# Forty-eight of the 128 half rows of the last up-projection slice, loaded as nine short transfers

## The chip, the cores and the metric

The kernel runs on one core of one Trainium2 chip. The metric is the device time of one execution in microseconds, lower is better. The core has a matrix engine (PE, with weight loads shown as PEld), a vector engine (DVE), a scalar engine (ACT), a general engine (POOL), and a sequencer (SP) that issues nearly all transfers of this kernel. Transfers from HBM to the on-chip memory are carried out by 16 DMA engines. The on-chip memory has 128 partitions; the kernel holds one array, `space`, of 50,176 32-bit columns on every partition, and manages it by itself.

## The reference

Two attention blocks and two gated MLP blocks alternate, with the same weights both times, for a batch of two and one new token:

```
x = x + attention(layernorm(x))      # 32 heads of 128, 8192 cached keys and values per head, width 576
x = x + mlp(layernorm(x))            # h = gelu(x @ w_gate) * (x @ w_up);  h @ w_down;  inner width 4608
x = x + attention(layernorm(x))
x = x + mlp(layernorm(x))
```

All of it is float32. Keys and values are 537 MB together and are read in both attention blocks, except what is held on chip from one to the next. The second MLP, where the change lies, needs the 576 x 4608 matrices `w_gate` and `w_up` and the 4608 x 576 matrix `w_down`, 10.6 MB each.

## The kernel before, in words

**One queue of loads.** The function `plan_first`, `plan_mlp(0)`, `plan_second` and `plan_mlp(1)` write the list of all loads in the order in which they are to be issued. Each entry of the list, `queue`, is a function that looks for a place in `space` (class `Arena`) and, if there is one, issues the transfer on SP's queue; if not, it returns False and the list stops there. `done(key)` frees a place and calls `pump`, which goes on with the list. All this happens while the program is written, so that the order of the issues is fixed; on the chip SP waits, before each issue, until the last readers of the place are done. The method `Arena.fit` tries the end of the last place it gave, then a lower bound, then the ends of all places in use.

**Completion semaphores.** The transfers on SP's queue take eight completion semaphores in turn. Before a transfer is issued on a semaphore, SP waits until the transfer that had it before, eight issues earlier, has landed.

**The second MLP.** `plan_mlp(1)` puts these loads on the list behind the eight 128-row blocks of the second output projection (`wo`): `w_gate` in two transfers, `w_up` in four, `w_down` in seven. A weight matrix of 576 rows of 4608 is seen as 1152 half rows of 2304 values (9216 bytes). Partition `p` holds half rows `9p` to `9p + 8`; `half_rows` loads for all 128 partitions the slices `us` of these nine. `GU` says which: `w_gate` slices 0 to 4 and 5 to 8, `w_up` slices 0 to 2, 3 to 5, 6 and 7, and, alone, slice 8. That last one, the ninth half rows of the up projection, is one transfer of 128 rows of 9216 bytes.

**The products.** `norm` writes the normalised input to the tile `xt`, with 32 columns for each of the nine slices: a half row belongs to the first or the second half of the weight's columns, by whether partition and slice are even or odd, and the input stands once for each half (columns multiplied by `side`). `all_products` then goes through the slices in the order of the loads; for each slice it makes eight products, of eight columns of `xt` with 288 columns of the weight, which add up in the two banks of the accumulator `acc`. PE has to wait for each transfer as it comes to it. Then `activate` (scaling by `rstd`, a transpose, the gelu) is run for each of the two banks, and the products with `w_down` follow in the order of its seven transfers. Ahead of the first four of these, `idle_products` makes a few products whose results are not used. `add_to_x` and two small stores end the program.

```
GU = [[range(0, 5), range(5, NU)], [range(0, 3), range(3, 6), range(6, 8), single[-1]]]
...
nc.sync.dma_start(t.rearrange("p (u w) -> p u w", w=width), rows[:, us[0]:us[-1] + 1, :])
```

Of the kernel before, what the change touches and what calls it, by code (L numbers as in the profile page):

```python
# [11 lines left out]
ALU = mybir.AluOpType  # L12
AX = mybir.AxisListType
PSUM = bass.MemoryType.PSUM

P = 128
B = 2
# [4 lines left out]
DF = 4608  # L22
# [3 lines left out]
HALF = P // 2  # L26

GH = 4
NU = 9
EQ = 512  # L30
HG = DF // 16
PAD = 6
# [10 lines left out]
END = RING + NPLACE * PLACE  # L43
HELD = 5
SPLIT = (18, 18, 12, 16)
FOLD = 2


# [76 lines left out]
def decode_layers(ctx, tc, x_in, kc, vc, wq, wo, wg, wu, wd, out):  # L125
    nc = tc.nc
# [12 lines left out]
    for c in range(4):  # L139
        for s in range(2):  # L140
            lo = 32 * c + s * B
# [5 lines left out]
    arena = Arena()  # L147
    queue, ready, places = [], {}, {}

    def pump():  # L150
        while queue and queue[0]():
            queue.pop(0)

    def done(key):
        arena.free(key)
        pump()

    def part_at(at, n):
        return space[:, at:at + n]
# [62 lines left out]
    def by_rows(key, src, n, k, loaded):  # L222

        first, rows = sum(SPLIT[:k]), SPLIT[k]

# [24 lines left out]
    def half_rows(key, w, us, first):  # L250

        width = w.shape[1] // 2
        rows = w.rearrange("r (s w) -> (r s) w", w=width).rearrange("(p u) w -> p u w", p=P)

        def transfers(t):
            nc.sync.dma_start(t.rearrange("p (u w) -> p u w", w=width), rows[:, us[0]:us[-1] + 1, :])

        weights(key, len(us) * width, first, transfers)

    def of_half(h, k):  # L260

        width = wq.shape[1] // 2
        rows = wq.rearrange("r (s w) -> (r s) w", w=width).rearrange("(p u) w -> p u w", p=P)

        def transfers(t):
            for e in range(2):
                nc.sync.dma_start(t[e::2, :], rows[e::2, 2 * k + (h + e) % 2, :])

        weights(("wq", 1, h, k), width, None, transfers)
# [63 lines left out]
    GU = [[range(0, 5), range(5, NU)], [range(0, 3), range(3, 6), range(6, 8), single[-1]]]  # L333
# [87 lines left out]
    def plan_mlp(layer):  # L421
        if layer == 0:
            for h in range(2):
                for u in range(4):
                    split_rows("g", wg, h, u)
                split_middle(h)
                for u in range(4):
                    split_rows("u", wu, h, u)
        else:
            for g, (name, w) in enumerate((("g", wg), ("u", wu))):  # L430
                for us in GU[g]:
                    half_rows((name, layer, us[0]), w, us, 0)
        for rows in DOWN[layer]:
            down(layer, rows)

# [7 lines left out]
    ident = consts.tile([P, P], F32, name="ident")  # L443
# [48 lines left out]
    home = consts.tile([P, 3 * DH + 16], F32, name="home")  # L492
# [3 lines left out]
    xt = consts.tile([P, PAD + NU * 32], F32, name="xt")  # L496
# [3 lines left out]
    acc = psum1.tile([P, 2, 512], F32, name="acc")  # L500
# [12 lines left out]
    low = bank2[:, 2 * GH + P + 8:]  # L513
    share = low[:, :FOLD * JC]
    kept = psum1.tile([P, JC, DH], F32, name="kept")
# [15 lines left out]
    def small(p, n):  # L531

        if n > 2:
            return turned[0:p, 0:n]
        smalls.append(smalls.pop(0))
        return smalls[0][0:p, 0:n]
# [65 lines left out]
    def attention(layer):  # L602
# [75 lines left out]
        def split(n):  # L678

            return layer == 1 and n == SINGLE[1]  # L680

        def count(n, k, m):

            return SPLIT[k] if split(n) else m * JC

        def base(n, k):

            return sum(SPLIT[:k]) if split(n) else k * JC

# [17 lines left out]
        def multiply(n, k, m):  # L707
# [7 lines left out]
            if n == SINGLE[1] and k == 0 and layer == 0:  # L715
                rest = ready[key_of(n)][2].rearrange("p j d -> p (j d)")[:, (JC - SPLIT[2]) * DH:]
                for to, lo in (
# [143 lines left out]
        def weigh(n):  # L861

            lo = ITEMS[n].parts - FOLD
            pr = weights_of(n)[:, 2 * JC * lo:2 * JC * (lo + FOLD)].rearrange("p (g a e) -> p a g e", a=2, e=4)
            nc.vector.tensor_tensor(
                out=share.rearrange("p (g e) -> p g e", e=4), in0=pr[:, 0], in1=pr[:, 1], op=ALU.add
            )
            rows = FOLD * JC
            t = part_at(arena.live[name("v", layer, n), lo][0], FOLD * PART).rearrange("p (j d) -> p j d", d=DH)
            nc.vector.tensor_tensor(out=t, in0=t, in1=share.unsqueeze(2).to_broadcast([P, rows, DH]), op=ALU.mult)  # L870
# [4 lines left out]
        def folded(n):  # L875

            key, lo = name("v", layer, n), ITEMS[n].parts - FOLD
            nc.tensor.matmul(  # L878
# [198 lines left out]
    def mlp(layer):  # L1077
        split = layer == 0
        rstd = norm(split)
        if split:  # L1080
            idle_products(2, 1)
        hT = once.tile([P, 2, NI, 2, 2, B], F32, name="hT", tag="xc")

        def window(u, at):

            return xt[:, PAD + 32 * u - at:PAD + 32 * u - at + 4 * B]

        def split_products(h):

            steps = [(("g", layer, h, u), u, 2, (0,)) for u in range(4)] + [(("gu", layer, h), 4, 1, (0, 1))]  # L1090
            steps += [(("u", layer, h, u), u, 2, (1,)) for u in range(4)]
            for key, u, sides, gs in steps:
                w = ready.pop(key).rearrange("p (k c w) -> p k c w", c=4, w=HG)
                for k in range(2):
                    g, e = (k, 0) if u == 4 else (gs[0], k)
                    for c in range(4):
                        nc.tensor.matmul(
                            acc[32 * c:32 * c + 4 * B, h, :HG], window(u, 4 * g + 2 * e), w[:, k, c, :],
                            start=(key == steps[0][0] and k == 0), stop=(key == steps[-1][0] and k == 1),
                        )  # L1100
                done(key)
                if key != steps[-1][0]:
                    idle_products(1, None if h else 1)

        def all_products():

            for g, name in enumerate("gu"):
                for us in GU[g]:
                    w = ready.pop((name, layer, us[0])).rearrange("p (u v c w) -> p u v c w", v=2, c=4, w=HG)
                    for u in us:  # L1110
                        for v in range(2):
                            for c in range(4):
                                nc.tensor.matmul(
                                    acc[32 * c:32 * c + 4 * B, v, :HG], window(u, 4 * g), w[:, u - us[0], v, c, :],
                                    start=(g == 0 and u == 0), stop=(g == 1 and u == NU - 1),
                                )
                    done((name, layer, us[0]))

        def activate(v):

            o = acc[:, v, :HG]
            nc.scalar.activation(o, o, AF.Copy, scale=rstd)  # L1122
            gu = once.tile([P, NI, 32], F32, name="gu", tag="row")
            nc.vector.transpose(gu, o.rearrange("p (m i) -> p i m", i=NI))  # L1124
            g = gu[:, :, 0:4]
            a = once.tile([P, NI, 4], F32, name="ga", tag="part")
            nc.vector.tensor_mul(a, g, g)
            nc.vector.tensor_scalar(a, a, 0.044715, 1.0, op0=ALU.mult, op1=ALU.add)
            nc.vector.tensor_mul(a, a, g)
            nc.scalar.activation(a, a, AF.Tanh, scale=math.sqrt(2.0 / math.pi))  # L1130
            nc.vector.scalar_tensor_tensor(a, a, 1.0, g, op0=ALU.add, op1=ALU.mult)
            nc.vector.tensor_mul(a, a, gu[:, :, 4:8])
            a, to = a.rearrange("p i (e b) -> p (i e) b", b=B), hT[:, v].rearrange("p i e s b -> p (i e) s b")
            nc.vector.tensor_scalar_mul(to[:, :, 0, :], a, 0.5)
            nc.scalar.mul(to[:, :, 1, :], a, 0.5)

        if not split:
            all_products()
        for v in range(2):
            if split:  # L1140
                split_products(v)
            activate(v)
        for n, rows in enumerate(DOWN[layer]):
            if n < len(IDLE[layer]):
                idle_products(IDLE[layer][n], 0)
            w = ready.pop(("d", layer, rows[0])).rearrange("p (i c) -> p i c", c=D)
            for k, (t, i) in enumerate(rows):
                v, e = divmod(t, 2) if split else (t % 2, t // 2)
                for c in range(4):
                    nc.tensor.matmul(  # L1150
                        xps[32 * c:32 * c + 2 * B, :], hT[:, v, i, e, :, :].rearrange("p s b -> p (s b)"),
                        w[:, k, c * CW:(c + 1) * CW],
                        start=(rows is DOWN[layer][0] and k == 0), stop=(t, i) == (NT - 1, NI - 1),
                    )
            done(("d", layer, rows[0]))
        add_to_x()
        if layer == 0:
            idle_products(1)
# [34 lines left out]
```

## Time and profile before

| | |
|---|---|
| median of three runs | 2683.82 us (2683.8 to 2685.11) |
| the profiled execution's own time | 2683.47 us |
| its span, from the first to the last instruction | 2681.7 us |
| bytes read | 1152.39 MB, 430 GB/s over the span |
| DVE, POOL, PE, ACT busy | 76%, 58%, 34%, 6% of the span |
| last load landed | about 2677.9 us after the start of the span |

The profile consists of a page (busy time of the engines, the span in 40 slices, DMA queues, the chain of work that ended last, groups of instructions, transfers) and of views that answer for any window of time: a timeline of instructions with the idle time before each and what ended it, the waits of an engine or of SP's queue, and tables by window. In the tables by window the column "DMA share" is the busy share of the 16 DMA engines, so that 1/16 or 0.06 is one engine. A row of the timeline gives the start, the duration, the engine, the line, what is written and read, the shape and the count, and in brackets the idle time before it. A wait is inferred from semaphores. The time of a run and the span differ by some 1.8 us that lie around the span.

### The profile page before, as it was taken

Reading aid. Unit: us, or ns where it says so; the run is one execution under the profiler, and the core shown is the slowest. Engines: PE = TensorE matmul, PEld = TensorE weight load, DVE = VectorE, ACT = ScalarE, POOL = GpSimd, SP = SyncE. Lnnn points to the kernel's source line nnn. Section 1 sums busy time; section 2 is a strip of 40 time slices with the busy share of each in tenths; the row PEclk is TensorE's granted clock in tenths of the full one; section 3 lists DMA queues with packets and bytes.
Section 4 is the critical chain, followed back from the end, with each engine's and each line's share of the span. In section 5 each row is a group of like instructions: output and inputs, shape, how many; then the busy total and the mean of one; then the engine's idle time right before and its main releaser. Section 6 shows DMA issues by size and latency. Waiting matters only on the chain. (4 is left out here: it accounts for less than half of the span.)

```text
span 2681.7 us, 16126 instructions
## 1 busy us (share of the span) xinstructions
PE 912.3 (34%) x6484; PEld 288.9 (11%) x6484; DVE 2027.3 (76%) x979; ACT 166.9 (6%) x797; POOL 1551.8 (58%) x408
## 2 busy tenths in 40 slices
PE   1323332233233233334663333223323323332346
PEld 0100010010001000111221101001000100010012
DVE  4878888888888888867037878888888888888740
ACT  0000000000000000000026000000000000000000
POOL 2546676667666766744028457666766666676520
PEclk8656655665566566566986665566566556655678
DMA  9999999999999999999999999999999999999998
GB/s 422 437 434 428 435 434 433 431 433 433 434 432 434 430 436 434 428 431 427 417 414 426 436 434 429 434 435 434 431 431 435 432 433 434 433 430 436 430 426 382
DMA packets 31498, 1153.44 MB, mean 430 GB/s; under 512 B 3880, under 2 KB 3904, under 8 KB 5696
## 3 DMA queue, kind: packets, MB, share of 16 engines
q1 hardware_dynamic: 31384, 1152.40, 99.8%
q8 instruction: 51, 0.84, 0.1%
q14 instruction: 23, 0.19, 0.0%
q10 hardware_dynamic: 40, 0.01, 0.0%
HBM read 1152.39 MB, written 0.00 MB: 430 GB/s over the span
## 5 line engine op out<-in xcount | busy, mean ns | idle before, releaser
L767 POOL TENSOR_TENSOR space<-space 128x3072 f32<-128x3072 f32 (+4 forms) x221 | 1127.8, 5103 | 474.8 <-DVE space L738 335.1
L738 DVE TENSOR_TENSOR space<-space,bank 128x6144 f32<-128x6144 f32 (+4 forms) x223 | 1111.8, 4987 | 300.4 <-DMA space<-in_A_k_cache_dram 230.6
L770 DVE TENSOR_REDUCE scores<-space 128x48 f32<-128x3072 f32 (+4 forms) x223 | 569.3, 2553 | 91.9 <-POOL space L767 91.7
L873 POOL TENSOR_TENSOR space<-space 128x2048 f32<-128x2048 f32 x144 | 390.0, 2708 | 385.7 <-DVE space L870 362.3
L899 PE MATMUL acc<-space,prz 128*8 128x512 f32 x3328 | 509.6, 776 | 206.6 <-DMA space<-in_A_v_cache_dram 202.5
L653 PE MATMUL bank<-qsb,pick 4*64 4x128 f32 (+1 forms) x256 | 45.4, 432 | 850.9 <-DVE space L738 843.3
L870 DVE TENSOR_TENSOR space<-space,bank 128x4096 f32<-128x4096 f32 x48 | 212.2, 4420 | 1.6
L899 PEld LDWEIGHTS acc<-space,prz 128*8 128x8 f32 x3328 | 98.7, 107 | 559.4 <-issue 356.8
L819 ACT ACTIVATE nbs<-bank 128x2 f32<-128x2 f32 (+1 forms) x68 | 11.6, 171 | 1812.4 <-PE bank L804 1782.8
L921 PE MATMUL bank<-of,wide 128*32 128x2 f32 x512 | 40.9, 202 | 237.9 <-DVE wide L914 237.9
L653 PEld LDWEIGHTS bank<-qsb,pick 4*64 4x64 f32 (+1 forms) x256 | 20.3, 200 | 872.3 <-DVE space L738 855.5
L796 PE MATMUL bank<-ident,m 128*1 128x128 f32 x68 | 21.7, 319 | 242.5 <-DVE m L794 242.3
L575 POOL TENSOR_TENSOR rstd<-ve,mhalf 128x1 f32<-128x1 f32 x4 | 2.2, 550 | 176.0 <-DVE ve L573 176.0
L878 PE MATMUL acc<-space,owner 128*8 128x512 f32 x96 | 89.9, 1039 | 0.0
L1124 DVE STREAM_TRANSPOSE gu<-acc 128x288 f32<-128x288 f32 x4 | 1.9, 483 | 93.2 <-ACT acc L1122 93.2
L921 PEld LDWEIGHTS bank<-of,wide 128*32 128x32 f32 x512 | 35.7, 154 | 326.1 <-DVE wide L914 324.9
L835 PE MATMUL bank<-sums,unit 128*128 128x2 f32 x120 | 35.2, 363 | 86.9 <-ACT prz L827 86.9
L913 DVE TENSOR_TENSOR acc<-acc,diag 128x512 f32<-128x512 f32 x64 | 43.5, 679 | 27.6 <-PE acc L899 27.6
L940 ACT ACTIVATE oT<-bank,rinv 32x8 f32<-32x8 f32 x110 | 28.5, 259 | 381.5 <-PE bank L921 380.8
L827 ACT ACTIVATE prz<-scores,nbs 64x128 f32<-64x128 f32 (+1 forms) x128 | 50.7, 396 | 17.2 <-POOL prz L817 14.4
L760 ACT ACTIVATE space<-space 128x128 f32<-128x128 f32 x164 | 48.4, 296 | 19.4 <-DVE space L738 16.5
L804 PE MATMUL bank<-m,unit 1*128 1x2 f32 (+1 forms) x136 | 38.5, 350 | 25.6 <-DVE m L802 25.6
(100 smaller groups left out, 519.0 us busy)
## 6 DMA issues: line engine op xcount, KB each, us to landing
space<-in_A_k_cache_dram SPq DMA_DIRECT2D x6, 4096.0 KB
space<-in_A_v_cache_dram SPq DMA_DIRECT2D x5, 4096.0 KB
space<-in_A_wo_dram SPq DMA_DIRECT2D x15, 1152.0 KB
space<-in_B_w_gate_dram SPq DMA_DIRECT2D x16, 576.0 KB
space<-in_B_w_up_dram SPq DMA_DIRECT2D x16, 576.0 KB
space<-in_B_w_down_dram SPq DMA_DIRECT2D x8, 1152.0 KB
space<-in_A_v_cache_dram SPq DMA_DIRECT2D x4, 2048.0 KB
space<-in_A_wq_dram SPq DMA_DIRECT2D x16, 512.0 KB
```

The costliest lines, as they stand in the source:

```text
L653: nc.tensor.matmul(qb[n][to, :], pick[32 * c:32 * c + 4, r:r + 1].to_broadcast([4, P // it.heads]), qsb[32 * c:32 * c + 4, (h % 4) * DH:(h ...
L738: nc.vector.tensor_tensor(out=u[:, :r, :], in0=t[:, :r, :], in1=qb[n].unsqueeze(1).to_broadcast([P, r, DH]), op=ALU.mult)
L760: nc.scalar.activation(u[:, j, :], u[:, j, :], AF.Copy, accum_out=S[n][:, base(n, k) + j:base(n, k) + j + 1])
L767: nc.gpsimd.tensor_tensor(out=half, in0=half, in1=u[:, :r, DH // 2:], op=ALU.add)
L770: nc.vector.tensor_reduce(out=S[n][:, base(n, k):base(n, k) + own_rows(n, k, m)], in_=prod.pop((n, k)), axis=AX.X, op=ALU.add)
L827: nc.scalar.activation(pr[at, lo:].rearrange("p (g e) -> p g e", e=4)[:, 0:it.rows // 2:2, :], s[at, :it.rows].rearrange("p (g r) -> p g r ...
L870: nc.vector.tensor_tensor(out=t, in0=t, in1=share.unsqueeze(2).to_broadcast([P, rows, DH]), op=ALU.mult)
L873: nc.gpsimd.tensor_tensor(out=t[:, :rows], in0=t[:, :rows], in1=t[:, rows:2 * rows], op=ALU.add)
L878: nc.tensor.matmul(accumulator(n)[0:8, :], owner.rearrange("p a e -> p (a e)"), part_at(arena.live[key, lo][0], 4 * DH), start=False, stop ...
L899: nc.tensor.matmul(accumulator(n)[32 * c:32 * c + 8, :], pr[:, at:at + 8], t[g // 4][:, g % 4 * 4:g % 4 * 4 + 4, :].rearrange("p j d -> p ...
L913: nc.vector.tensor_tensor(out=q, in0=q, in1=diag.unsqueeze(2).to_broadcast([P, 4, DH]), op=ALU.mult)
L921: nc.tensor.matmul(po[lo:lo + 32, i, :], t[:, i::GH], of, start=True, stop=True)
```

## The change

The ninth half rows of the second up projection are no longer one transfer of 128 rows. Their place in `space` gets twice the columns and 65 more (4673 instead of 2304), and is asked for earlier, right behind the first `w_gate` transfer.

- **Nine short transfers**, six of six rows and three of four rows, take 48 rows, all of odd partitions: the rows 3, 5 and 7 of each group of eight. 44 of these go to another partition, 0 to 63, into a second block of columns (`low`): row `i` of a transfer goes to partition `to + 4 i`. The other four (103, 111, 119, 127) go where they went before. Three of these transfers are issued ahead of each of three large ones: the second `w_gate` transfer and the first two of `w_up`.
- **Two further transfers**, 64 rows (the even partitions) and 16 rows (partitions 1, 9, ..., 121), take the other 80, ahead of the third `w_up` transfer.
- **The input moves along.** `move_down`, after `norm`, builds from pieces of the identity a 128 x 64 matrix (`perm`, in the last 65 columns of the new place) that moves the input of the 44 rows to their new partitions, multiplies it on PE with the input, and copies the result to spare columns of `xt`; a second spare block gets the input with the moved rows set to zero.
- **The products.** `ninth_products` replaces the eight products of slice 8 by sixteen, eight over 128 partitions and eight over 64. The order of the slices in the products stays.

```
+EARLY = 6
...
+    def ninth_rows(key, w, u):
+
+        width = w.shape[1] // 2
+        rows = w.rearrange("r (s w) -> (r s) w", w=width).rearrange("(q u) w -> u q w", u=NU)[u]
+
+        def make():
+            at = arena.fit(key, 2 * width + HALF + 1, 0)
...
+        def some(lo, step, n, to=None):
+            at = slice(lo, lo + step * (n - 1) + 1, step)
+            if to is None:
+                return piece(lambda home, low: nc.sync.dma_start(home[at, :], rows[at, :]))
+            there = slice(to, to + 4 * n - 3, 4)
+            return piece(lambda home, low: nc.sync.dma_start(low[there, :], rows[at, :]))
+
+        queue.append(make)
+        short = [some(8 * EARLY * a + 3 + 2 * k, 8, EARLY, HALF // 2 * a + k) for a in range(2) for k in range(3)]
+        short += [some(99, 8, 4, 3), some(101, 8, 4, HALF // 2 + 3), some(103, 8, 4)]
+        return short, [some(0, 2, HALF), some(1, 8, 16)]
...
-            for g, (name, w) in enumerate((("g", wg), ("u", wu))):
-                for us in GU[g]:
-                    half_rows((name, layer, us[0]), w, us, 0)
+            half_rows(("g", 1, GU[0][0][0]), wg, GU[0][0], 0)
+            short, rest = ninth_rows(("u", 1, NU - 1), wu, NU - 1)
+            for us, name, w in ((GU[0][1], "g", wg), (GU[1][0], "u", wu), (GU[1][1], "u", wu), (GU[1][2], "u", wu)):
+                for piece in short[:3] or rest:
+                    piece()
+                short = short[3:]
+                half_rows((name, 1, us[0]), w, us, 0)
...
+        def move_down():
+
+            at = PAD + 32 * (NU - 1)
+            perm, here = [ready["u", layer, NU - 1][:, DF + lo:DF + hi] for lo, hi in ((0, HALF), (HALF, HALF + 1))]
+            nc.vector.memset(perm, 0.0)
+            for a in range(2):
+                to = perm[:, HALF // 2 * a:HALF // 2 * a + 4 * EARLY].rearrange("p (c i) -> p c i", i=4)
+                of_ident = ident[:, 8 * EARLY * a:8 * EARLY * (a + 1)].rearrange("p (c e) -> p c e", e=8)
+                nc.scalar.copy(to[:, :, 0:3], of_ident[:, :, 3::2])
+                nc.scalar.copy(to[:, 0:4, 3], ident[:, 96:P].rearrange("p (c e) -> p c e", e=8)[:, :, 3 + 2 * a])
+            moved = small(HALF, 2 * B)
+            nc.tensor.matmul(moved, perm, xt[:, at:at + 2 * B], start=True, stop=True)
+            nc.scalar.copy(xt[:HALF, at + 12:at + 16], moved)
+            nc.vector.reduce_sum(here, perm, axis=AX.X)
+            nc.vector.tensor_scalar(here, here, -1.0, 1.0, op0=ALU.mult, op1=ALU.add)
+            nc.vector.tensor_scalar_mul(xt[:, at + 20:at + 24], xt[:, at:at + 2 * B], here)
+
+        def ninth_products():
...
+            for v in range(2):
+                for c in range(4):
+                    to = acc[32 * c:32 * c + 4 * B, v, :HG]
+                    nc.tensor.matmul(to, xt[:, at + 16:at + 24], w[:, 0, v, c, :], start=False, stop=False)
+                    nc.tensor.matmul(to, xt[:HALF, at + 8:at + 16], w[:HALF, 1, v, c, :], start=False, stop=True)
...
         if not split:
+            move_down()
             all_products()
```

More of the change, by code (lines that the diff above doesn't have):

```diff
@@ L258, in half_rows, with piece, run @@
         weights(key, len(us) * width, first, transfers)
+    def ninth_rows(key, w, u):
[3 more added lines that the diff above has]
+            at = arena.fit(key, 2 * width + HALF + 1, 0)
+            if at is None:
+                return False
+            ready[key] = part_at(at, 2 * width + HALF + 1)
+            return True
+        def piece(issue):
+            def run():
+                t = ready[key]
+                issue(t[:, :width], t[:, width:2 * width])
+                return True
+            return lambda: queue.append(run)
+        def some(lo, step, n, to=None):
[8 more added lines that the diff above has]
+        return short, [some(0, 2, HALF), some(1, 8, 16)]
     def of_half(h, k):
@@ L1103, in split_products @@
                     idle_products(1, None if h else 1)
+        def move_down():
[14 more added lines that the diff above has]
+        def ninth_products():
+            key, at = ("u", layer, NU - 1), PAD + 32 * (NU - 1)
+            w = ready.pop(key)[:, :DF].rearrange("p (s v c w) -> p s v c w", s=2, v=2, c=4)
+            for v in range(2):
[3 more added lines that the diff above has]
+                    nc.tensor.matmul(to, xt[:HALF, at + 8:at + 16], w[:HALF, 1, v, c, :], start=False, stop=True)
+            done(key)
         def all_products():
@@ L1108, in all_products @@
                 for us in GU[g]:
+                    if (g, us[0]) == (1, NU - 1):
+                        ninth_products()
+                        continue
                     w = ready.pop((name, layer, us[0])).rearrange("p (u v c w) -> p u v c w", v=2, c=4, w=HG)
@@ L1114, in all_products @@
                                     acc[32 * c:32 * c + 4 * B, v, :HG], window(u, 4 * g), w[:, u - us[0], v, c, :],
-                                    start=(g == 0 and u == 0), stop=(g == 1 and u == NU - 1),
+                                    start=(g == 0 and u == 0), stop=False,
                                 )
```

## The prediction, made before the changed kernel was run

> **What bounds the kernel now.** First the page: its second part (busy tenths) and its third (queues).
>
> ```profile
> DMA  9999999999999999999999999999999999999998
> DMA packets 31498, 1153.44 MB, mean 430 GB/s; under 512 B 3880, under 2 KB 3904, under 8 KB 5696
> q1 hardware_dynamic: 31384, 1152.40, 99.8%
> ```
>
> The 16 DMA engines are busy for 99.8% of the span, so nothing but the transfers sets the time, and the change moves not a byte less. What is left to gain lies at the end, where the engines stop one after the other. The table by windows shows it (columns: window, length, busy time of PE, PEld, DVE, ACT and POOL, PE's granted clock, DMA share, GB/s):
>
> ```profile
> 2671.00:2672.00 1.00, 0.50 (x18) 0.44 (x22) 0.00 (x0) 0.00 (x0) 0.00 (x0) 1.00 0.99 396
> 2672.70:2673.40 0.70, 0.70 (x32) 0.61 (x26) 0.00 (x0) 0.00 (x0) 0.00 (x0) 1.00 0.76 313
> 2673.40:2674.10 0.70, 0.70 (x24) 0.43 (x17) 0.00 (x0) 0.00 (x0) 0.00 (x0) 1.00 0.62 257
> 2674.80:2675.50 0.70, 0.23 (x4) 0.00 (x0) 0.00 (x0) 0.00 (x0) 0.00 (x0) 1.00 0.54 221
> 2675.50:2676.20 0.70, 0.43 (x16) 0.38 (x20) 0.00 (x0) 0.00 (x0) 0.00 (x0) 1.00 0.62 237
> 2676.90:2677.60 0.70, 0.42 (x16) 0.33 (x16) 0.00 (x0) 0.00 (x0) 0.00 (x0) 1.00 0.10 40
> ```
>
> One engine is 0.0625 of the share. Until 2672 all 16 work; then 0.76 is twelve, 0.62 ten, 0.54 nine. So four engines have done their part by about 2672.7, two more by 2673.7, one by about 2675, and nine go on to between 2676 and 2677.8: four engines are about 5 us ahead of the last one, two about 4 us. All carry the same 8 rows of every 128-row transfer; the late ones lost time earlier. Then the timeline of the end:
>
> ```profile
> 2644.71 5.20 PE L1113 MATMUL acc<-space,xt 128*8 128x288 f32 x48 [5.11 <-DMA space<-in_B_w_up_dram]
> 2650.19 2.13 PE L1113 MATMUL acc<-space,xt 128*8 128x288 f32 x32 [0.28 <-DMA space<-in_B_w_up_dram]
> 2652.99 1.16 PE L1113 MATMUL acc<-space,xt 128*8 128x288 f32 x16 [0.67 <-DMA space<-in_B_w_up_dram]
> ...
> 2671.50 2.39 PE L1150 MATMUL bank<-space,hT 128*4 128x144 f32 x72 [1.55 <-DMA space<-in_B_w_down_dram]
> ...
> 2675.77 0.92 PE L1150 MATMUL bank<-space,hT 128*4 128x144 f32 x24 [0.74 <-DMA space<-in_B_w_down_dram]
> 2677.18 1.14 PE L1150 MATMUL bank<-space,hT 128*4 128x144 f32 x24 [0.49 <-DMA space<-in_B_w_down_dram]
> 2677.89 0.43 PE L1150 MATMUL bank<-space,hT 128*4 128x144 f32 x8
> 2678.39 0.31 DVE L579 TENSOR_TENSOR x<-bank,x 128x144 f32<-128x144 f32 x1 [18.90 <-PE bank L1150]
> 2678.72 0.65 SPq L1165 DMA_DIRECT2D out_dram<-x  x1
> ```
>
> PE waits for nearly every transfer, the last too: the end is the slowest engine's last row (landed by 2677.89, when the last eight products, also counted in the row above, start), then 3.8 us of products, addition and store up to 2681.7.
>
> **The change, part by part.**
>
> *The rows' engines.* How many engines does a transfer of six rows use? The transfers with few rows here are `x` and `out`:
>
> ```profile
> q10 hardware_dynamic: 40, 0.01, 0.0%
> x<-in_A_x_dram ACTq DMA_DIRECT2D x8, 1.1 KB
> out_dram<-x ACTq DMA_DIRECT2D x1, 2.2 KB
> ```
>
> On that queue 40 packets are eight transfers of two rows and one of four if each row is a packet and each used engine adds one closing packet: 8 x (2 + 2) + (4 + 4) = 40. (The page's 3880 packets under 512 B agree: 241 issues x 16, plus 16, 4 and 4.) So rows go to as many engines as there are rows, one each, and I take six rows to use six engines and four rows four. 64 rows use all 16, four rows each, as the interleaved halves of the first MLP do, and 16 rows one each. Before, each engine had 8 ninth rows. After: 64/16 + 16/16 = 5 on every engine; besides, 6 + 3 = 9 on four engines and 6 on two. Four engines get 14 (+6), two get 11 (+3), ten get 5 (-3).
>
> *The price of a row.* 430 GB/s over 16 engines is 26.9 GB/s, so 9216 bytes take 0.343 us. Ten engines gain 3 x 0.343 = 1.03 us, four lose 2.06, two lose 1.03.
>
> *Which engines those are* the profile does not number. If the four and the two are the early ones, the four have 5 - 2.06 = 2.9 us left before the old end, the two 4 - 1.03 = 3.0, and the old end itself moves by **-1.03 us**. If the late ones are loaded, the end moves by +2.06 us. I take the first: the share falls by just four engines and then two, and lasting differences of this kind belong to engines, not to rows. [...]
>
> *Nine small transfers in the place of one.* Could each hold its engines for a time of its own? The nearest rows are the first MLP's half transfers, 64 rows each (window 1285 to 1330):
>
> ```profile
> DMA packets 2964, 18.69 MB, mean 415 GB/s; under 512 B 568, under 2 KB 568, under 8 KB 1287
> q1 hardware_dynamic: 2960, 18.63, 100.6%
> ...
> space<-in_B_w_gate_dram SPq DMA_DIRECT2D x16, 576.0 KB
> space<-in_B_w_up_dram SPq DMA_DIRECT2D x14, 576.0 KB
> space<-in_B_w_gate_dram SPq DMA_DIRECT2D x4, 288.0 KB
> space<-in_B_w_up_dram SPq DMA_DIRECT2D x4, 288.0 KB
> ```
>
> 38 of them ran at 415 instead of 430 GB/s: 3.5% of 45 us, 1.6 us, or 0.04 us each at most, without a gap (100.6%). Nine cost 0.4 us, and only on early engines; the one added on the late ones 0.04. Term: 0, bounds 0 and +0.04. [...]
>
> *SP's queue and its eight semaphores.* Ten more issues. The interleaved pairs of the first MLP cost:
>
> ```profile
> 1284.90 1.20 SPq L277 DMA_DIRECT2D space<-in_B_w_gate_dram  x2
> ```
>
> 0.6 us each, so 6 us of SP time. What matters is that each issue waits for the landing of the eighth before it. Today's issues and waits (second block: waits in 2640 to 2655):
>
> ```profile
> 2589.38 8.96 SPq L256 DMA_DIRECT2D space<-in_B_w_up_dram  x4
> 2620.54 30.00 SPq L300 DMA_DIRECT2D space<-in_B_w_down_dram  x7
> ```
> ```profile
> SPq L300 <- DMA space<-in_B_w_up_dram: 12.9, 2, 7.8
> 2644.73 5.81 SPq L300 DMA_DIRECT2D space<-in_B_w_down_dram  x2
> ```
>
> The last two `w_down` issues wait for landings of `w_up`, eight issues back, although their place is free: the rule is visible. With the short transfers in line, the first `w_up` (u0) comes eight behind the first `w_gate` (g0) and is issued when that lands, at 2617.4 by the row below, 28 us later than now. Then g1, 4608 KB, is in flight, 10.9 us at 430 GB/s, and three short ones; an issue takes under 2 us to move data (store: issued 2678.72, all over by 2681.7). The early engines run 5 us ahead, so they end g1 and shorts at about 2617.4 - 5 + 10.9 + 2 = 2625: 6 us to spare. The second `w_up` waits for g1's landing (about 2628.3) with u0's 8.2 us behind it: the early engines are done at about 2634.5, 4 us to spare. The first `w_down` waits for u0 (2636.5) with some 15 us in flight; the later ones have more. No engine runs dry: 0 us. With under 2 us left in any of these it would cost what is missing, one to one.
>
> *The place in `space`.* 4673 columns do not fit above g0 (35072 to 46592 of 50176), so the place is 16128 to 20801, free when three parts of the last values are read; g1 follows at 20801, u0 and u1 go to 0 and 6912 after `wo` blocks, the third to 30017. The third `w_down` misses the end by one column (44993 + 5184 = 50177) and goes into g1's place, as now. All of these are free before the semaphore that SP waits for: 0.
>
> *`move_down`* runs on DVE, ACT and PE here:
>
> ```profile
> 2608.59 0.11 DVE L573 TENSOR_SCALAR ve<-mv 128x1 f32<-128x1 f32 x1
> 2608.79 0.55 POOL L575 TENSOR_TENSOR rstd<-ve,mhalf 128x1 f32<-128x1 f32 x1 [38.01 <-DVE ve L573]
> 2617.47 7.10 PE L1113 MATMUL acc<-space,xt 128*8 128x288 f32 x80 [10.38 <-DMA space<-in_B_w_gate_dram]
> L735 ACT COPY qs<-bank 128x128 f32<-128x128 f32 x5 | 1.2, 248 | 0.5 <-ACT qsb L964 0.5
> ```
>
> A memset (0.15), four copies (0.25 each by the last row), a product (0.4), a copy (0.25), three small DVE instructions (0.5): 2.3 us, 3 with the handovers, before a wait of 8.8 us for g0. Hidden; uncovered it would cost 3 us.
>
> *The order of the products.* Now the 32-product `w_up` slice lands last, at 2652.9 - 1.03 = 2651.9, and has 32 + 16 products behind it (2.13 + 1.16 by the rows) instead of 16: `activate` starts 1.05 us later than now while the loads come 1.03 earlier, so PE needs 2.1 us of slack. It idles 1.55 + 0.74 + 0.49 = 2.78 us before the last transfers. Cover with 0.7 us to spare; without it PE sets the end, at up to +1.05.
>
> Sum: **-1.03 us**. The profiled execution (span 2681.7, time 2683.47, 1.8 around it) would take 2682.4; the median of the runs is 0.35 above it, so 2683.82 - 1.03 = **2682.8 us**.
>
> **The rivals.**
>
> *A, no gain.* PE becomes the bound through the later `activate`, or the code of the changed program is fetched once more on a late engine:
>
> ```profile
> q8 instruction: 7, 0.11, 0.5%
> ```
>
> Seven fetches in the window 2583 to 2682 take 0.5% of 16 x 98.7 us, 1.1 us each. Either takes back the gain: 2683.4 to 2685. The clearest cover, 0.7 us, is thin. The same holds if six rows are spread over all engines, so that nothing moves: 2683.8.
>
> *B, the wrong engines.* The short transfers' engines are among the nine late ones: +2.06, 2685.9. It decides as soon as one of the four is less than 2.06 us ahead of the last engine. Against it: four and two match the steps of the share.
>
> *C, the pieces wait for each other.* They write interleaved partitions of the same columns; if SP waited for one to land before the next, each group of three adds two landings of 1.7 us (the final store needs about that) during which SP issues nothing large; as the following large transfer is then late by up to 4 us in four groups, the stream stands for about 12 us: 2695. Against it: the pair at 1284.90, two interleaved halves in 1.20 us, without a wait between.
>
> *D, more gain.* The ten engines also drop a fetch: 2681.7.
>
> **How the numbers follow.** Forecast 0.63; A 0.17; B 0.09; C 0.07; D 0.04. 0.2%, 5.4 us, is about what a measurement of this kernel tells from no change; forecast, A, B and D lie inside. Slower by more takes C or an unseen stall: 0.08; faster by more has no mechanism: 0.01; within: 0.91. The range takes in forecast, A and B, with a fetch less at the low end: 2681.6 to 2686.0; the forecast alone 2682.2 to 2683.4.
>
> **What would show it.** In the windows of the end, the DMA share stays near 1 longer (the step to twelve moves from 2672.7 to about 2674.7) and falls to 0.10 about 1 us earlier. The last products' wait is still on `w_down`. `w_up` is issued at about 2617.4 and 2628.3, with a DMA share of 1 from 2612 to 2669. `move_down` is over by 2612. Wrong: a share under 0.95 in that stretch (C), PE without idle time before the last 24 products (A), or the same end with the early engines finished later (B).

## The result: slower, and the profile after

The changed kernel takes **2703.14 us** (median of 6 runs, 2702.09 to 2704.23) against 2683.86 us (2683.33 to 2685.11, 6 runs) of the kernel before: a ratio of **1.0071, 95% interval 1.0058 to 1.0084**, 19.3 us more. The prediction was 2682.8 us, with a range up to 2686.0. The profiled execution took 2702.33 us, with a span of 2700.5 us.

First the page, its second and third part. The last digit of the busy tenths is 6 where it was 8, and the share of the weights' queue is 99.1% where it was 99.8%. 99.8% of 2681.7 us and 99.1% of 2700.5 us are both 2676 us: the DMA engines are busy as long as before, and the 19 us more are time in which they wait.

```profile
DMA  9999999999999999999999999999999999999996
DMA packets 31562, 1153.44 MB, mean 427 GB/s; under 512 B 3944, under 2 KB 3968, under 8 KB 5760
q1 hardware_dynamic: 31448, 1152.40, 99.1%
```

Where that time lies, the table by windows of the changed kernel shows (window, length, busy time of PE, PEld, DVE, ACT, POOL, PE's clock, DMA share, GB/s):

```profile
2583.00:2612.00 29.00, 16.41 (x322) 8.85 (x314) 4.32 (x13) 0.00 (x0) 0.55 (x1) 0.85 1.02 432
2612.00:2645.00 33.00, 0.00 (x0) 0.00 (x0) 0.00 (x0) 0.00 (x0) 0.00 (x0) 0.50 1.00 417
2645.00:2669.00 24.00, 19.81 (x278) 7.69 (x278) 0.60 (x3) 0.68 (x5) 0.00 (x0) 0.83 0.82 326
2669.00:2680.00 11.00, 8.22 (x29) 1.32 (x28) 1.63 (x7) 0.96 (x4) 0.00 (x0) 1.00 0.98 414
2680.00:2700.00 20.00, 16.11 (x302) 8.20 (x302) 1.94 (x8) 0.81 (x3) 0.00 (x0) 0.91 0.05 18
```

The same two middle windows of the kernel before:

```profile
2612.00:2645.00 33.00, 16.25 (x196) 6.00 (x200) 0.00 (x0) 0.00 (x0) 0.00 (x0) 0.76 0.99 424
2645.00:2669.00 24.00, 19.33 (x251) 7.32 (x244) 3.27 (x14) 1.77 (x6) 0.00 (x0) 0.77 1.01 428
```

While `w_gate` and `w_up` land, from 2612 to 2645, PE does **nothing at all**; before, it worked off 16 us there. The transfers go on (share 1.00). From 2649.2 to 2669 PE works without a pause, and now the transfers pause (0.82). In 2669 to 2680 PE is busy for 8.22 us with 29 records of products (the views count each of these products as two), and after 2680 it runs for another 16 us although hardly a byte arrives. The timeline names the instructions:

```profile
2606.86 0.11 DVE L1146 MEMSET space<- 128x64 f32 x1
...
2648.62 0.21 ACT L1150 COPY space<-ident 128x18 f32<-128x18 f32 x1 [74.36 <-DMA space<-in_B_w_up_dram]
...
2649.19 0.38 PE L1153 MATMUL bank<-xt,space 128*64 128x4 f32 x2 [43.91 <-ACT space L1151]
...
2649.50 18.55 PE L1181 MATMUL acc<-space,xt 128*8 128x288 f32 x272
...
2654.00 7.64 SPq L333 DMA_DIRECT2D space<-in_B_w_down_dram  x7
...
2667.87 0.65 PE L1166 MATMUL acc<-space,xt 128*8 128x288 f32 x2
...
2668.45 0.65 PE L1167 MATMUL acc<-space,xt 64*8 64x288 f32 x2
...
2669.03 0.65 PE L1166 MATMUL acc<-space,xt 128*8 128x288 f32 x2
...
2677.32 0.47 ACT L1190 ACTIVATE acc<-acc,rstd 128x288 f32<-128x288 f32 x1 [27.55 <-PE acc L1167]
```

Three things are to be read here.

1. `move_down` (L1146 to L1157) begins at 2606.86 as foreseen, but its **second instruction**, ACT's first copy into `perm`, starts at 2648.62, 41.6 us after the memset has ended. The waits put it down to a transfer of `w_up`, the nine, 64 and 16 rows being in that group. In the trace's semaphore records the 16-row transfer has its last landing at 2648.32, 0.3 us before the copy.
2. The small product of `move_down` (L1153) needs the copies, and PE starts none of the products with `w_gate` and `w_up` ahead of it, although the first `w_gate` transfer has its last landing at 2616.51: PE stands idle for 43.91 us. Then they run in one piece from 2649.50. SP's next `w_down` transfer in turn needs the place that PE's first products read, and is issued at 2654.00 (its wait stands below the list).
3. The sixteen ninth products, 128 and 64 partitions in turn, start one after the other at intervals of **0.58 us** (2667.87, 2668.45, 2669.03): some 9.3 us to 2677.2, where eight products of 128 partitions took 1.16 us before.

SP's waits for PE ahead of the `w_down` issues (us in total, times, longest):

```profile
SPq L333 <- PE acc L1181: 22.2, 4, 17.6
```

### The profile page after: what moved, and what is told of

It reads as the page before. It is cut to its first block, busy times and chain, and to the rows that moved or that the text cites. A ratio compares the mean times of both kernels' runs of the same rounds, so it can differ in the third digit from the quotient of the medians.

```text
span 2700.5 us, 16188 instructions
## 1 busy us (share of the span) xinstructions
PE 913.8 (34%) x6502; PEld 289.1 (11%) x6502; DVE 2028.1 (75%) x983; ACT 167.7 (6%) x802; POOL 1552.2 (57%) x408
## 3 DMA queue, kind: packets, MB, share of 16 engines
q1 hardware_dynamic: 31448, 1152.40, 99.1%
```

## The experiments

All times stand against the runs of the kernel before on the same chip. The letters of the theories hold within one expectation only. An interval of 0.001 on either side of a ratio is 2.7 us.

### The matrix in another tile

```
-            perm, here = [ready["u", layer, NU - 1][:, DF + lo:DF + hi] ...]
+            perm, here = [scores[:, lo:hi] for lo, hi in ((0, HALF), (HALF, HALF + 1))]
```

> Edit: the 65 columns of the moving matrix lie in the tile `scores`, not beside the transferred rows in `space`. Theory W (three separate causes: the first copy of move_down waits until the last piece of the ninth rows has landed, at 2648.3 in the changed kernel's trace, and PE with it; the sixteen products that alternate 128 and 64 rows take 9.3 us instead of 1.2; the short transfers load engines that are not the early ones, about +1 us): the copies run at once, PE starts at 2616.6 when the first w_gate transfer lands, the ninth products still take 9.3 us behind the last w_up landing (about 2653.6 + 2.1 + 9.3 = 2665), and with the 23.2 us that the changed kernel takes from there to its end the time is about 2690 to 2691. Rival S (the short transfers and the waits for their semaphores slow the stream itself): the first w_down issue stays at about 2654 and the time at about 2703.

Measured: 2691.65 us against 2683.68, ratio 1.0031 (1.0019 to 1.0043): +8.0 instead of +19.3. PE's rows of this kernel:

```profile
2609.38 0.38 PE L1153 MATMUL bank<-xt,scores 128*64 128x4 f32 x2 [2.30 <-ACT scores L1151]
2616.89 6.37 PE L1181 MATMUL acc<-space,xt 128*8 128x288 f32 x80 [7.13 <-DMA space<-in_B_w_gate_dram]
```

`move_down`'s product now runs at 2609.38, and then PE waits 7.13 us for the first `w_gate` transfer (`g0`), as it waited for it before. The wait of the copies cost about 11 of the 19 us.

### The products in two groups

```
-            for v in range(2):
-                for c in range(4):
-                    (128 partitions, then 64 partitions, onto the same columns)
+            for k in range(2):
+                for v in range(2):
+                    for c in range(4):
+                        (k = 0: 128 partitions; k = 1: 64 partitions)
```

> Edit: of the sixteen ninth products the eight over 128 partitions come first, then the eight over 64; nothing else. Theory W: the sixteen take about 2.3 us instead of 9.3, the wait of move_down stays, so about 7 us less than the changed kernel: 2696. Rival S: the time is set by the stream, 2703 as before the edit.

Measured: 2696.14 us against 2683.68, ratio 1.0048 (1.0034 to 1.0061): +12.5, 6.8 us less than the changed kernel, as expected.

### Both

> Edit: both of the two edits before. Theory W: only the third cause is left, the loads set the end again: 2684.5 to 2685, 0.6 to 1 us above the kernel before. The forecast on record (short transfers load the early engines): 2682.8. Rival S: about 2703.

Measured: 2685.36 us against 2683.68 (11 and 19 runs), ratio 1.0007 (0.9998 to 1.0016). The two losses explain 17.6 of the 19.3 us. The sixteen products of this kernel:

```profile
2657.25 1.14 PE L1168 MATMUL acc<-space,xt 128*8 128x288 f32 x16
2658.32 1.15 PE L1170 MATMUL acc<-space,xt 64*8 64x288 f32 x16
```

They take 2.2 us instead of 9.3. What is left, +1.7 us, is near what these runs can tell, and on the wrong side of the forecast's -1.03. The next runs go after the two causes and then after this rest.

### The place or the form of the write?

The copy that waited writes columns of `perm` that no transfer writes. Is it the place, the same tile as the landing rows, or the form, every fourth column left out? Here `perm` is built in `scores` and goes to its old place by one copy of 64 whole columns:

```
-            nc.vector.memset(perm, 0.0)
+            made = scores[:, :HALF]
+            nc.vector.memset(made, 0.0)
...
+            nc.scalar.copy(perm, made)
```

> The 64 columns of the matrix are built in another tile and then written to their old place by one copy of whole rows. Theory F, the scattered columns of ACT's copies are what ties them to the landing of the short transfers: as with the matrix in the other tile, 2691.6 us (2690.4 to 2693). Rival P, the place itself does, behind the same two blocks as the landing rows: 2703 us, with ACT idle until about 2648.

Measured: 2693.09 us against 2683.38, ratio 1.0036 (1.0022 to 1.0051). ACT's rows:

```profile
2610.34 0.21 ACT L1151 COPY scores<-ident 128x18 f32<-128x18 f32 x1 [34.84 <-DVE scores L1147]
...
2610.94 0.24 ACT L1153 COPY space<-scores 128x64 f32<-128x64 f32 x1
```

The write to the very same place starts at 2610.94 without waiting for the landings, and the loss is 9.7 us instead of 19.3 (just above the range expected of theory F). So the **form** is the cause: in the compiled program the scattered copy of the changed kernel waits on six semaphores of transfers, the whole copy on one and the memset on one. It looks as if the scattered columns were taken to touch more than they write, the landing rows included; how the program decides that wasn't looked into.

### Why do the alternating products cost 0.58 us?

Two things change from one of them to the next: it adds to the same columns of `acc` as the one before, and it reads another number of partitions. The first alone, in the kernel before, on the third `w_up` slice (two half rows):

```
+                    if (g, us) == (1, GU[1][2]):
+                        order = [(u, v, c) for v in range(2) for c in range(4) for u in us]
```

> The kernel before, with the 16 products of the third w_up slice (two half rows) in pairs onto the same columns of acc, all over 128 partitions. Theory C, two products in a row onto the same 32 columns of PE lose the overlap: the slice takes 8 x 0.58 = 4.6 us instead of 2.13, and the time 2683.7 to 2686. Rival R, the change between 128 and 64 partitions from product to product is what costs: 2.13 us, 2683.7 us.

Measured: 2683.37 us against 2683.38 (ratio 1.0000, 0.9990 to 1.0010), and the slice:

```profile
2648.87 2.15 PE L1114 MATMUL acc<-space,xt 128*8 128x288 f32 x32 [0.72 <-DMA space<-in_B_w_up_dram]
```

2.15 us, as before: same columns twice in a row cost nothing. The second alone, in the kernel with the matrix in the other tile: 128 and 64 partitions still alternate, but neighbours go onto different columns.

```
+            for n in range(9):
+                if n < 8:   (128 partitions onto column group n)
+                if n:       (64 partitions onto column group n - 1)
```

> The matrix in the other tile, and the sixteen ninth products alternate between 128 and 64 partitions, but a product over 64 partitions follows one onto other columns than its own. Theory C (same columns twice in a row cost): 2.3 us for the sixteen, 2685.4 us as with the products in two groups. Rival R (the change of the number of partitions costs): 9.3 us for the sixteen, 2691.6 us as with the alternating pairs.

Measured: 2692.25 us against 2683.38, ratio 1.0032 (1.0017 to 1.0048), with these rows:

```profile
2659.35 0.65 PE L1167 MATMUL acc<-space,xt 128*8 128x288 f32 x2
2659.93 0.65 PE L1170 MATMUL acc<-space,xt 64*8 64x288 f32 x2
2660.51 0.65 PE L1167 MATMUL acc<-space,xt 128*8 128x288 f32 x2
```

Again 0.58 us from start to start. It is the **change of the number of partitions**, at each step, that costs: 0.58 us a product instead of 1.16 / 8 = 0.145. 0.58 is four times 0.145; why the change costs that much, no run shows.

### Every row at home

Are the other partitions needed at all? The same eleven transfers, each row to its own partition, with no `move_down` and the old eight products:

```
-            there = slice(to, to + 4 * n - 3, 4)
-            return piece(lambda home, low: nc.sync.dma_start(low[there, :], rows[at, :]))
+            return piece(lambda home, low: nc.sync.dma_start(home[at, :], rows[at, :]))
...
-            move_down()
```

> Edit: the same eleven transfers in the same order, but every row to its own partition, with 2304 columns, no move_down and the eight products of the kernel before. Theory W: the loads alone, 2684.5 to 2685. The forecast on record: 2682.8. [...] Rival S: near 2703.

Measured: 2690.96 us against 2683.68, ratio 1.0027 (1.0016 to 1.0038): +7.3 us. A miss: I had taken the moved partitions for a detail. The table by windows of this kernel:

```profile
2612.00:2645.00 33.00, 16.86 (x173) 5.75 (x176) 0.00 (x0) 0.00 (x0) 0.00 (x0) 0.71 0.98 364
2645.00:2669.00 24.00, 13.02 (x122) 3.81 (x115) 3.25 (x14) 1.70 (x6) 0.00 (x0) 0.71 1.01 408
```

The DMA engines are as busy as before (0.98, 1.01) but move 364 and 408 GB/s instead of 424 and 428. By (424 - 364) / 424 x 33 + (428 - 408) / 428 x 24 that is 4.7 + 1.1 = 5.8 of the 7.3 us: slower packets, not a gap.

The uneven load could be a part of it. So the next kernel has it even: all 128 rows at home in eight transfers of 16 rows, 8 rows on each engine as before (in the changed kernel's trace a transfer of 16 rows has 16 landings, as one of 128 rows has).

```
+        return [some(k, 8, 16) for k in (1, 3, 5, 7, 0, 2)], [some(4, 8, 16), some(6, 8, 16)]
...
+                for piece in short[:2] or rest:
```

> All 128 ninth rows in eight transfers of 16 rows, each row to its own partition, two ahead of each of the four large transfers; no matrix, the old eight products. Every engine carries 8 rows, as before. Theory W, a row written to partitions that the other engines' rows also go to takes about 0.7 us instead of 0.34 (seen where every row stayed at home): 8 x 0.36 = 2.9 us, 2686.6 us, up to 2691 if the large transfers are slowed too, and fewer GB/s at a DMA share of 1 from 2612 to 2645. Rival L, only the uneven load of the engines costs: 2683.7 us (2683 to 2684.5).

Measured: 2693.60 us against 2683.50, ratio 1.0037 (1.0024 to 1.0051): +10.1. There is a loss with the even load too, but it is well above the 2.9 us of the rows alone, and the time above the 2691 us given for slowed large transfers.

```profile
2612.00:2645.00 33.00, 13.54 (x148) 4.64 (x152) 0.00 (x0) 0.00 (x0) 0.00 (x0) 0.71 0.99 324
2645.00:2669.00 24.00, 14.43 (x145) 4.57 (x138) 2.31 (x9) 1.30 (x4) 0.00 (x0) 0.71 0.99 382
```

324 and 382 GB/s at a share of 0.99: 7.8 + 2.6 = 10.4 us, all of the loss, and the large transfers that stand beside the small ones are slowed with them. The trace's semaphore records give each engine's landing, without its number: the second `w_gate` transfer (`g1`) takes 13.1 us here from the last landing before it to its own, and 10.9 us in the kernel before. With the moved partitions the kernel with both mends has 410 and 415 GB/s:

```profile
2612.00:2645.00 33.00, 16.41 (x192) 5.58 (x192) 0.00 (x0) 0.00 (x0) 0.00 (x0) 0.76 0.98 410
2645.00:2669.00 24.00, 16.43 (x189) 5.71 (x190) 3.26 (x14) 1.77 (x6) 0.00 (x0) 0.75 1.00 415
```

So the partitions to which a short row goes matter. One transfer shows it inside this same kernel: of the three transfers of four rows, two go to moved partitions and the third (103, 111, 119, 127) stays at home. On their four engines the second lands 0.35 to 0.45 us behind the first, and the third 0.70 to 0.78 us behind the second. The six-row transfers, all moved, land 0.33 to 0.36 us apart.

Why the partitions matter is not shown: no run here names the engine of a row, and none tries another spacing of the rows than `to + 4 i`. What theory W of the run with sixteens says of the other engines' rows was the author's guess; the measured part of it is the 0.70 to 0.78 us.

### The rest: which engines carry the short rows

In the kernel with both mends, without the nine short transfers (their rows left out):

```
-                for piece in short[:3] or rest:
+                for piece in () if short else rest:
```

> The kernel with both mends (matrix in the other tile, products in two groups), without the nine short transfers: their 48 rows are left out of the computation. Every engine carries 5 rows. Theory B, the last engine of that kernel carries short rows, 11 in all: 6 x 0.343 = 2.06 us less than 2685.4, 2683.3 us. Forecast's theory, the last engines carry 5 rows with and without them: no change, 2685.4 us.

Measured: 2684.39 us against 2683.50 (11 and 15 runs), ratio 1.0003 (0.9994 to 1.0012): +0.9, between the two expectations. Its profile, of an execution of 2686.09 us, shows why it doesn't decide:

```profile
2670.00:2675.00 5.00, 5.00 (x88) 2.42 (x80) 0.00 (x0) 0.00 (x0) 0.00 (x0) 1.00 0.78 321
2675.00:2680.00 5.00, 5.00 (x135) 3.29 (x137) 0.00 (x0) 0.00 (x0) 0.00 (x0) 1.00 0.17 66
```

PE is busy without a pause up to the end, so PE, not the last landing, sets this end. It is the same in the kernel with both mends. There PE's last wait for a transfer is the one for the third `w_up` slice, and nothing is waited for before the last products:

```profile
2653.82 3.60 PE L1184 MATMUL acc<-space,xt 128*8 128x288 f32 x32 [2.68 <-DMA space<-in_B_w_up_dram]
...
2677.08 2.37 PE L1222 MATMUL bank<-space,hT 128*4 128x144 f32 x66
```

The cover that the prediction gave to the order of the products is gone: the sixteen products of that slice (32 records) and then the sixteen ninth products stand between the last `w_up` landing and `activate`. The slice is slower, too. In the table by windows, the kernel before and then the one with both mends, PE's granted clock is 1.00 and 0.55:

```profile
2650.20:2652.30 2.10, 2.10 (x32) 0.77 (x32) 0.00 (x0) 0.00 (x0) 0.00 (x0) 1.00 1.07 456
2653.80:2657.20 3.40, 3.38 (x32) 1.16 (x36) 0.00 (x0) 0.00 (x0) 0.00 (x0) 0.55 1.03 439
```

Ahead of this slice PE had stood idle for 0.28 us in the first kernel and for 2.68 us in the second, in which the 64 and 16 rows land before it. In the run with two products in a row onto the same columns the pause was 0.72 us and the slice took 2.15 us. No run varies the pause alone.

So two runs with the sixteen products ahead of that slice, as the rows land, one with all rows and one without the nine transfers:

```
                     if (g, us[0]) == (1, NU - 1):
+                        continue
+                    if g == 1 and us == GU[1][2]:
                         ninth_products()
-                        continue
```

> The kernel with both mends, with the sixteen ninth products ahead of the third w_up slice's instead of behind them, as the rows land. Theory P, in the kernel with both mends PE sets the end along with the loads: the activation starts about 2.3 us earlier, PE idles again before the last w_down products, and the time is 0.5 to 1 us less than 2685.4: 2684.4 to 2684.9 us. Rival L, the loads alone set the end: 2685.4 us, though PE idles.

> As e11_ninth_first, without the nine short transfers: their 48 rows are left out of the computation. With PE out of the way the last landing alone counts. Theory B, the last engine carries 11 rows with the short transfers and 5 without: 1.6 to 2.06 us less than e11_ninth_first, 2682.5 to 2683.2 us. Forecast's theory, the last engines carry no short rows: the same time as e11_ninth_first. Besides, if the 64 and 16 rows cost as much as 128 rows in one transfer (2.6 and 2.79 us in the landings so far), five rows on each engine gain nothing against the kernel before: 2683.5 us or more.

Measured against 2683.97 us (21 runs): with all rows 2685.03 us, ratio 1.0004 (0.9996 to 1.0013), +1.1; without the nine transfers **2683.51 us**, ratio 0.9998 (0.9989 to 1.0007), -0.5. Nine of the eleven times without them (up to 2684.18) lie below the lowest of the eleven with them (2684.36). In the first of the two PE pauses again before its last products:

```profile
2655.20 2.13 PE L1185 MATMUL acc<-space,xt 128*8 128x288 f32 x32 [0.63 <-DMA space<-in_B_w_up_dram]
...
2673.75 2.39 PE L1223 MATMUL bank<-space,hT 128*4 128x144 f32 x72 [1.29 <-DMA space<-in_B_w_down_dram]
...
2677.95 0.92 PE L1223 MATMUL bank<-space,hT 128*4 128x144 f32 x24 [0.67 <-DMA space<-in_B_w_down_dram]
2679.30 1.14 PE L1223 MATMUL bank<-space,hT 128*4 128x144 f32 x24 [0.43 <-DMA space<-in_B_w_down_dram]
```

The slice takes 2.13 us again, with a pause of 0.63 us ahead of it. With PE out of the way the nine transfers cost 1.5 us (0.7 to 2.2, if the eleven times of each are resampled), where 11 rows against 5 on the last engine would be 2.06. The semaphore records say the same in single executions: from the last landing of `g0` to the last landing of all it takes 60.5 us in the kernel before, 62.8 with both mends and 61.2 without the nine (1.6 less), 63.2 and 61.4 in the pair above (1.8 less). And in the kernel with both mends the engine that lands **last** of `g1`, at 2627.75, is followed 0.34, 0.36 and 0.35 us later by the last short landings of that group (2628.09, 2628.45, 2628.80). It carries short rows, and 11 ninth rows in all, not 14: the four-row transfers, which follow the first `w_up` transfer, have landed on their engines by 2637.00, and the last landing of that transfer is at 2637.28. The same is seen in the kernel with the sixteen products first (2629.08, then 2629.43, 2629.77 and 2630.13). In the profile of the changed kernel, another engine lands last of `g1`.

## Why the prediction was wrong, step by step

**`move_down`, the step that failed most.** The prediction hid its 2.3 to 3 us before an 8.8 us wait. The work itself was priced high enough: with the matrix in another tile it takes 1.4 us and is over by 2610.0, with PE waiting for `g0` until 2616.89. But it looked only at the engines, and asked nothing of where the matrix lies: in the place that transfers in flight are still writing. The copy waited for them, 41.6 us beyond its time, with PE's whole queue behind it. About 11 of the 19.3 us. The prediction named rival C, pieces that wait for each other's landing because they write interleaved parts of one tile, and looked for it on SP's queue alone. SP waited for none of it (the three short issues at 2585.95, 2588.69 and 2591.48 came before any had landed); ACT waited for the landings, until 2648.62.

**The order of the products.** Two errors. The sixteen products were priced at 1.16 us by a row of eight products (16 records) that all have 128 partitions. Alternating they take 9.3 us, grouped 2.2. That is 6 to 7 of the 19.3 us. And the slack of 2.78 us was weighed against a need of 2.1, where the true need, with both mends, was larger. The sixteen take 2.2 us, and in that execution the third `w_up` slice ahead of them took 3.4 us from 2653.8: its 2.13 us had been read at a granted clock of 1.00, and here the clock was 0.55. So the sixteen ended at 2659.5, where the old eight ended at 2654.15. Rival A's "PE becomes the bound" was true of what was left, for some 0.6 us by the medians (less than they can tell; PE's pauses in the rows are the evidence).

**Which engines.** The prediction took the short transfers' engines for the early ones (-1.03) and gave the other case, B, a chance of 0.09. B is nearer to what the runs show: the nine transfers cost 1.5 us in the end rather than nothing, and in two profiles an engine with 11 rows lands last of `g1`. The six engines are no group of early ones. By the landings of `g0`, before any short row, they were 4.9, 4.6, 3.2, 2.1, 2.0 and 1.4 us ahead of the last engine in the changed kernel's profile, and 4.8, 4.1, 2.2, 2.0, 1.6 and 0.0 us in that of the kernel with both mends. So the steps of four and two in the DMA share matched the numbers of rows by chance, and an engine's lead isn't the same in every execution. In the trace of the kernel before, which engine is early was not to be read, so the even odds of an unknown would have been the better price.

**The price of a row.** 0.343 us holds for the 128-row transfers (the 32 rows of `g1` on each engine take 10.9 us in the kernel before) and for the six-row ones at moved partitions (0.33 to 0.36 us apart). It failed for the four short rows at home (0.70 to 0.78 us) and for the 64 and the 16 rows, also at home: together five rows on each engine, they took 2.2 to 2.6 us in the landings of five kernels instead of 1.72, so that the gain over the old 2.79 was 0.2 to 0.6 us and not 1.03. The kernel without the short rows agrees: -0.5 us, in an interval that holds 0 as well.

**Right:** one engine per row (six and four landings). **SP's queue:** `w_up` was to be issued at 2617.4 and 2628.3, and was at 2616.57 and 2627.50, with a DMA share of 1.00 up to 2645. What the queue lost, it lost to PE: the `w_down` issues at 2654.00. **The nine small transfers** show no cost of their own: 1.5 us is not more than the 2.06 us of their rows. With both mends the kernel stands at 2685.4 with all nine.

**All steps in a row**, each against the runs of the kernel before on its own chip: +19.3 us as changed; +8.0 with the matrix in another tile; +1.7 with the products in two groups as well; +1.1 with these ahead of the third `w_up` slice; -0.5 without the nine transfers. The first two steps are clear of the spread, the step from +1.7 to +1.1 is not.

## What to carry to other kernels

Before a step is called hidden, ask of each tile that it writes who else is writing into it, in which form the write is made (scattered columns or whole ones), and what stands behind the waiting instruction in its engine's queue: here 1.4 us of work held PE for 44. Put products over different numbers of partitions in groups (here 2.2 us for sixteen, 9.3 alternating), and take their price from a row that alternates as they do, at the clock that they will have (here one slice took 2.13 us at 1.00 and 3.4 us at 0.55). For a transfer of few rows, ask to which partitions the rows go: here a short row took 0.33 to 0.45 us at moved partitions and 0.70 to 0.78 us at home, and with all ninth rows at home in transfers of 16 rows the large `g1` took 13.1 us instead of 10.9.

## What the runs showed of the hardware

- Alternating products over 128 and 64 partitions take 0.58 us each instead of 0.145, whether a product goes to the columns of the one before or to others; changing once, between two groups of eight, costs nothing that can be seen (2.2 us for the sixteen, eight over 128 partitions having taken 1.16 us).
- The same sixteen products of the third `w_up` slice took 2.13 us at a granted clock of 1.00, after a pause of 0.28 us, and 3.4 us at 0.55, after a pause of 2.68 us.
- Rows of 9216 bytes in transfers of 16, sent to their own partitions, took the throughput from 424 to 324 GB/s while the DMA engines showed a busy share of 0.99 in both kernels: here the share didn't tell the speed, the column of GB/s beside it did.
- Short rows at moved partitions landed 0.33 to 0.45 us apart, near the 0.343 us of a row of a large transfer; at home they took 0.70 to 0.78 us. Ten issues more on SP's queue left the DMA share at 1.00 from 2612 to 2645.
